# Order of GpSimd work, loads and background pieces in a fused attention and FFT kernel

## The chip, the cores and the metric

The kernel runs on one core of a Trainium2 chip. The metric is the device time of one execution in microseconds; before the change it is 700.23 us, the median of three runs (699.89 to 700.64).

## The reference

Two independent results are concatenated. The first is a causal attention over four segments of 512 positions, 32 heads of 18, with a memory that is carried from segment to segment:

```python
logits = jnp.einsum("bhqd,bhkd->bhqk", qs, ks) * scale + mask
p = _softmax(logits, axis=-1)
a_dot = jnp.einsum("bhqk,bhkd->bhqd", p, vs)
pq = phi(qs)
num = jnp.einsum("bhld,bhde->bhle", pq, M)
den = jnp.einsum("bhld,bhd->bhl", pq, z)[..., None] + 1e-6
o = g * (num / den) + (1.0 - g) * a_dot
M = M + jnp.einsum("bhld,bhle->bhde", phi(ks), vs)
z = z + jnp.einsum("bhld->bhd", phi(ks))
```

and then `o @ wo` over all heads. The second result is a 2D real FFT of a 2048 x 576 array, a product with complex weights, and the inverse transform.

## The kernel before

The program is one stream of instructions per engine, in the order in which the Python code records them. First come the forward FFT, the projections of q, k and v with the middle of the FFT, and the inverse FFT; the last half, from about 350 us on, is the loop of `attention`, and all the edits lie there.

**The loop.** It has 133 steps t. A step handles one head of one segment: `k,hh=divmod(t,4)` makes groups of four heads k = 0 to 31, and eight groups (32 steps) are a segment g. In step t three things are interleaved on TensorE:

- `s1(t+11)`: the logits of a head eleven steps ahead, only for their row maxima. Matmuls L678, with the causal mask added by L691, reduced on VectorE (L686, L692).
- `s2(t)`: the logits of this head again, transposed and with the maxima subtracted in the matmul (L727, L731, L732, L736), and the exponentials on ScalarE into the tiles P[0], P[1], P[2] (L728, L733, L737).
- `pv`: the product of P with the values for the group of four heads before, in the second step of a group the blocks of P[0] and the last columns of P[1], in the fourth step the rest of P[1] and P[2] (L756).

**The zeros.** After the last head of a group, four `affine_select` on GpSimd (L741) put zeros above the causal diagonal, each on a 128 x 4 x 128 block of P.

**The maxima's parts.** In the first step of a group, `mpath(k+2)` takes the maxima of the group two further on, combines them (L704, L705) and splits them on GpSimd into two bf16 parts, the tile `mh` (L707, L708). In the second step TensorE transposes mh (L711), ScalarE copies the result (L714), and two steps after the split's step a small DMA in ScalarE's own instruction order (L717) writes it into two rows of the Q tile, where s2 will use it.

**Background pieces.** `bg` is a list of generators: first `late_setup`, which loads wo and splits it into a high part (copy on ScalarE, L649) and a low part `wol` (subtraction on GpSimd, L650); then for each later segment `den` (the denominators, L807, L810), `mixed` and `oproj`, the output projection of the segment before (L901, its PSUM copied by L903). `mixed` alternates two kinds: `combine` multiplies the stored outputs u by the spread reciprocals (a small matmul pb, L878, with the product on VectorE, L881 or L883), adds the memory's part on GpSimd (L884) and splits the sum (L863, L868); `mem1` computes the memory's numerator (matmul pn, L831, copied by L833) and multiplies it with a reciprocal (pb, L837, L838). pb, pn, the denominators and the output projection share one PSUM buffer named "post" during the loop. A step gives pieces twice: `run_bg(0)` early and `run_bg(1.2)` after pv. Each call adds its rate to an account and runs one piece if that holds one, so that a step has one piece, and one in five steps two.

**Loads.** They go through SyncE's one queue in the order of the code. `stack_dmas` loads Q and K of eight heads at a time (L660, L662), one entry of a list per step; `load_v` loads their values `vs` (L669); `pq_load` loads the rows of phi(q) for the memory (L801), for the first time in steps 16 to 20, and `den` of step 34 needs all five. Each DMA signals one of eight semaphores in turn, and a DMA's issue waits until the one before it on the same semaphore has landed.

Of the kernel before, what the change touches and what calls it, by code (L numbers as in the profile page):

```python
# [5 lines left out]
F32=mybir.dt.float32; F32R=mybir.dt.float32r  # L6
# [358 lines left out]
ORD=(4,0,1,2,3)  # L365
# [42 lines left out]
class ATT:  # L408
# [224 lines left out]
    def late_setup(s,cp):  # L633

        nc,io=s.nc,s.io; q=[]
        s.sel=cp.tile([96,5,126],BF,name="sel",bufs=1); nc.gpsimd.dma_start(s.sel,io["sel"].rearrange("p (t m) -> p t m",t=5))
        s.woh=cp.tile([128,5,576],F32R,name="woh",bufs=1); s.wol=cp.tile([128,5,576],F32R,name="wol",bufs=1)
        for t in (0,1,2,3,5,4,6):
            if t: yield
            if t<6:  # L640
                x=cp.tile([128,576],F32,name="ob"); q.append((t,x))
                nc.sync.dma_start(x,io["wo"][:,576*t:576*t+576])
            yield
            if t!=5: yield
            if len(q)>(t<6):
                u,x=q.pop(0)
                if u==5: nc.scalar.copy(s.wol[64:96,4],x[64:96]); continue
                r=128 if u<4 else 72
                nc.scalar.copy(s.woh[:,u],x)  # L649
                nc.gpsimd.tensor_tensor(s.wol[:r,u],x[:r],s.woh[:r,u].bitcast(F32),op=OP.subtract)  # L650
        yield
        yield from s.gates()
    def stack_dmas(s,n,qk):
# [65 lines left out]
    def s2(s,t):  # L719
        nc=s.nc; k,hh=divmod(t,4); n,qd=divmod(k,2); h=4*qd+hh  # L720
        Q,K=s.Qs[n%3],s.Ks[n%4]; tp=s.tp
        if hh==0: s.P[k]=[tp.tile([128,4,w],F32,name=f"P{i}") for i,w in enumerate((512,512,256))]
        P=s.P[k]
        q=lambda o: Q[:110,h,o:]
        kk=lambda j: K[:110,h,128*j:128*j+128]
        p0=s.ps.tile([128,512],F32,name="s2",tag="s2")
        nc.tensor.matmul(p0,kk(0),q(0),start=True,stop=True)  # L727
        nc.scalar.activation(P[0][:,hh],p0,AF.Exp,scale=SC)  # L728
        yield
        p1=s.ps.tile([128,512],F32,name="s2",tag="s2")  # L730
        nc.tensor.matmul(p1[:,:384],kk(1),q(128),start=True,stop=True)  # L731
        nc.tensor.matmul(p1[:,384:],kk(3),q(384),start=True,stop=True)  # L732
        nc.scalar.activation(P[1][:,hh],p1,AF.Exp,scale=SC)  # L733
        yield
        p2=s.ps.tile([128,256],F32,name="s2",tag="s2")
        nc.tensor.matmul(p2,kk(2),q(256),start=True,stop=True)  # L736
        nc.scalar.activation(P[2][:,hh],p2,AF.Exp,scale=SC)  # L737
        r=slice(0,4) if k<31 else (slice(0,3) if hh==2 else slice(3,4))
        if hh==3 or k==31 and hh==2:
            def sel(x):  # L740
                nc.gpsimd.affine_select(out=x[:,r],in_=x[:,r],pattern=[[0,r.stop-r.start],[1,128]],compare_op=OP.is_ge,fill=0.0,base=0,channel_multiplier=-1)  # L741
            sel(P[0][:,:,:128])
            sel(P[1][:,:,:128])
            sel(P[1][:,:,384:])
            sel(P[2][:,:,:128])
        yield
    def pv(s,k,jj):

# [91 lines left out]
        yield  # L840
    def mixed(s,g):

        c=s.combine(g-1)
        d=5 if g==3 else 4
        for i in range(5+d):
            next(c,None); yield
            if i>=d:
                for _ in s.mem1(g,ORD[i-d]): yield
    def ux_load(s,g,t):
        r=126 if t<4 else 72  # L850
        s.ux[t]=s.tp.tile([128,512],F32,name="ux",tag="ux",bufs=3)
        s.nc.sync.dma_start(s.ux[t][:r],s.uD[g][126*t:126*t+r])
    def combine(s,g):
# [19 lines left out]
        for t in range(7+late):  # L873
            if t>1 and not late: high(ORD[t-2]); low(ORD[t-2])
            if t<5:
# [3 lines left out]
                if g==0:  # L879
                    s.am[t]=tp.tile([126,512],F32,name="am",bufs=5)  # L880
                    nc.vector.tensor_tensor(s.am[t][:r],x[:r],pb[:r],op=OP.mult)  # L881
                else:
                    nc.vector.tensor_tensor(x[:r],x[:r],pb[:r],op=OP.mult)  # L883
                    eng().tensor_tensor(s.am[t][:r],x[:r],s.am[t][:r],op=OP.add)  # L884
# [54 lines left out]
    def begin(s,sm,sp,ps1):  # L939
        s.late=[]; s.now=-1  # L940
        s.sm,s.sp,s.ps1=sm,sp,ps1
        s.mh=sm.tile([128,8,16],BF,name="mh",bufs=1); s.nc.gpsimd.memset(s.mh,0.0)
        s.mg={};s.mx={};s.m2={};s.P={};s.vs={};s.rc={};s.am={};s.pq={};s.ux={};s.potag=None
    def prologue(s):

        nc,io=s.nc,s.io
# [18 lines left out]
    def attention(s,tp,ps):  # L965
# [7 lines left out]
        q=[]  # L973
# [11 lines left out]
        for t in range(133):  # L985
            k,hh=divmod(t,4); n,qd=divmod(k,2); g=k//8
            if hh==0 and qd==0:
                if 0<n<14: q+=s.stack_dmas(n+2,0)
                if 0<n<13: q+=s.stack_dmas(n+3,1)
                if n+2<16: q.append(lambda n=n: s.load_v(n+2))  # L990
            st=t%32
            if 16<=t<21: s.pq_load(1,ORD[t-16])
            if t==34: bg.append(s.den(1,lane))
            if st==8 and g>0:
                def ln(g=g):
# [18 lines left out]
            steps(a,1)  # L1014
            steps(b,1)
            if 4<=t-1<132: s.pv((t-5)//4,(t-5)%4)
            run_bg(1.2)
            steps(a,1)
            if hh==1 and m is not None: steps(m,1)
            steps(b,1)  # L1020
            if hh==1 and m is not None: steps(m,1)
            if hh==0 and k+2<32: m=s.mpath(k+2); next(m)
            if t>=7 and t%4==3:
                s.pv_out((t-7)//4)
                if t%8==3:
# [155 lines left out]
```

## Time and profile before

| | |
|---|---|
| median of three runs | 700.23 us |
| profiled execution | 701.5 us, its span on the core 699.8 us |
| attention loop and tail | about 350 us to the end |
| GpSimd's selects L741 | 132, 78.2 us in all |

The span is the time from the first to the last instruction in the trace; the rest of an execution's time lies around it. Engines: PE is TensorE, PEld its weight loads, DVE VectorE, ACT ScalarE, POOL GpSimd, SP SyncE; a "q" behind a name means the engine's issuing of a DMA. Idle time of an engine is put down to what ended it. The profile models where a matmul ends, so matmuls that follow each other overlap.

### The profile page before, as it was taken

What the parts mean: (1) busy time and instruction counts of PE and PEld (TensorE: products, weight loads), DVE (VectorE), ACT (ScalarE), POOL (GpSimd) and SP (SyncE); (2) the same over time, 40 slices, a digit from 0 to 9 for tenths busy, and PEclk for the clock granted to TensorE, in tenths of its full rate; (3) what the DMA queues carried; (4) which work ended last, traced back from release to release, by engine and by line L of the source; (5) the groups of instructions that cost most, each with busy time, mean ns of one, the idle gap of its engine ahead of it and who ended that gap; (6) DMA issues with size and microseconds to landing.
All of it is one profiled execution on the core that took longest, in us unless ns stands there. A gap on an engine that the chain in (4) does not pass through costs nothing.

```text
span 699.8 us, 14371 instructions
## 1 busy us (share of the span) xinstructions
PE 680.0 (97%) x5040; PEld 501.9 (72%) x5040; DVE 537.7 (77%) x1149; ACT 445.3 (64%) x997; POOL 192.3 (27%) x389
## 2 busy tenths in 40 slices
PE   8999899999999999999999899999999999998998
PEld 5999679879879879999954455445666445663497
DVE  5898989789689679798588788888667876567633
ACT  4786695584684574545387687777656776567531
POOL 2111000100200101665135343443323652235310
PEclk9999999999999999999999999999999999999999
DMA  9895355594465778999348876986666776442142
GB/s 335 279 316 179 111 162 190 154 268 155 130 191 190 171 213 297 206 231 250 130 124 193 182 172 153 197 196 161 148 141 166 200 161 154 101 132 67 29 152 90
DMA packets 71362, 123.81 MB, mean 177 GB/s; under 512 B 12236, under 2 KB 39530, under 8 KB 67698
## 3 DMA queue, kind: packets, MB, share of 16 engines
q1 hardware_dynamic: 64638, 106.89, 58.0%
q0 software_dynamic: 5632, 15.76, 8.3%
q8 instruction: 40, 0.66, 0.4%
q10 hardware_dynamic: 1020, 0.25, 0.2%
q14 instruction: 32, 0.26, 0.1%
HBM read 82.10 MB, written 39.81 MB: 174 GB/s over the span
## 4 chain that ended last, share of the span: by engine, by line
PE 83%; DVE 6%; DMA 3%; ACT 3%; POOL 2%; issue 2%; ACTq 0%; SPq 0%; DVEq 0%; POOLq 0%
PE pj L485 15%; PE s L678 10%; PE pv L756 10%; PE pjv L485 9%; PE po L901 6%; PE i L318 4%; PE i L329 4%; PE s L727 3%; PE f L145 3%; PE s L731 3%; PE c L166 3%; PE po L930 2%; PE s L691 2%; PE pn L831 2%; PE pm L553 2%
## 5 line engine op out<-in xcount | busy, mean ns | idle before, releaser
L686 DVE CUSTOM_DVE_ANT_0 junk<-s,x 128x512 bf16<-128x512 f32 x248 | 137.0, 552 | 56.0 <-PE s L678 50.9
L741 POOL TENSOR_SCALAR_AFFINE_SELECT P<-P 128x512 f32<-128x512 f32 (+2 forms) x132 | 78.2, 623 | 112.4 <-ACT P L728 104.6
L692 DVE TENSOR_REDUCE mx<-s 128x4 f32<-128x512 f32 x128 | 87.7, 685 | 6.2 <-PE s L691 3.9
L728 ACT ACTIVATE P<-s 128x512 f32<-128x512 f32 x128 | 77.9, 609 | 12.3 <-PE s L727 3.4
L756 PE MATMUL pv<-P,vs 128*32 128x512 f32 (+3 forms) x1024 | 82.5, 439 | 0.1
L737 ACT ACTIVATE P<-s 128x256 f32<-128x256 f32 x128 | 50.0, 391 | 46.3 <-PE s L736 46.0
L733 ACT ACTIVATE P<-s 128x512 f32<-128x512 f32 x128 | 77.8, 608 | 2.5 <-PE s L732 2.2
L678 PE MATMUL s<-Ks,Qs 108*128 108x384 bf16 (+3 forms) x256 | 69.2, 301 | 1.5 <-DVE mx L692 1.2
L756 PEld LDWEIGHTS pv<-P,vs 128*32 128x32 f32 x1024 | 26.9, 109 | 45.3 <-issue 34.9
L485 PE MATMUL pj<-x,wqkh 128*128 128x512 f32 x162 | 56.4, 408 | 0.0
L230 DVE TENSOR_TENSOR Z<-Z 128x580 f32<-128x580 f32 (+2 forms) x51 | 45.6, 911 | 0.5
L678 PEld LDWEIGHTS <-Qs 108*128 108x128 bf16 x320 | 31.5, 98 | 19.3 <-issue 9.2
L691 PE MATMUL s<-tri,idb 128*128 128x128 bf16 x256 | 43.0, 219 | 0.0
L543 POOL MEMSET vt<- 128x32 f32 x16 | 2.3, 161 | 139.1 <-PE pm L553 127.8
L318 PE MATMUL i<-civ,Y 128*128 128x256 f32 (+1 forms) x288 | 39.2, 288 | 0.2 <-POOL Y L303 0.2
L318 PEld LDWEIGHTS i<-civ,Y 128*128 128x128 f32 (+1 forms) x288 | 36.6, 181 | 0.9 <-POOL Y L303 0.4
L329 PE MATMUL i<-itab,T 128*128 128x290 f32 (+1 forms) x224 | 36.6, 306 | 0.1
L485 PEld LDWEIGHTS pj<-x,wqkh 128*128 128x128 f32 x162 | 30.4, 189 | 8.5 <-issue 2.0
L485 PE MATMUL pj<-xh,wqkl 128*128 128x512 f32 x90 | 35.6, 395 | 0.0
L485 PE MATMUL pj<-xh,wqkh 128*128 128x512 f32 x90 | 35.6, 395 | 0.0
L485 PE MATMUL pj<-x,wqkl 128*128 128x512 f32 x90 | 35.5, 395 | 0.0
L504 DVE SCALAR_TENSOR_TENSOR ex<-pj,ex 128x512 f32<-128x512 f32 (+1 forms) x28 | 19.3, 689 | 20.2 <-ACT ex L502 20.1
(216 smaller groups left out, 1805.9 us busy)
## 6 DMA issues: line engine op xcount, KB each, us to landing
qkD<-sp SPq DMA_DIRECT2D x32, 384.0 KB
xin<-xb SPq DMA_DIRECT2D x16, 384.0 KB
cfw<-cfw POOLq DMA_DIRECT2D x16, 384.0 KB, 5.5
civ<-civ POOLq DMA_DIRECT2D x16, 384.0 KB, 9.7
vs<-vD SPq DMA_DIRECT2D x16, 330.0 KB
vD<-vt SPq DMA_DIRECT2D x16, 311.0 KB
W<-w SPq DMA_DIRECT2D x16, 290.0 KB
yb<-yout SPq DMA_DIRECT2D x16, 290.0 KB
```

The source lines that it names most:

```text
L318: nc.tensor.matmul(p[:m,k],Y[i][:,q,c*128:c*128+m],cc[:,hl,o:o+256],start=n==0,stop=n==5)
L329: nc.tensor.matmul(p,x,t,start=n==0,stop=n==6)
L485: s.nc.tensor.matmul(out,a,b,start=i==0,stop=i==len(L)-1)
L678: nc.tensor.matmul(out,Q[:108,h,128*i:128*i+128],K[:108,h,:128*(i+1)],start=True,stop=True)
L686: nc.vector.tensor_tensor_reduce(out=junk[:,:w],in0=src,in1=s.mask[:,512-w:],scale=1.0,scalar=-3.0e38, op0=OP.add,op1=OP.max,accum_out=s.m ...
L691: nc.tensor.matmul(pa[:,o+w-128:o+w],s.idb,s.tri,start=False,stop=True,skip_group_check=True)
L692: nc.vector.tensor_reduce(out=s.mx[k][:,hh],in_=pa.rearrange("p (b c) -> p b c",c=128),axis=mybir.AxisListType.X,op=OP.max)
L728: nc.scalar.activation(P[0][:,hh],p0,AF.Exp,scale=SC)
L733: nc.scalar.activation(P[1][:,hh],p1,AF.Exp,scale=SC)
L737: nc.scalar.activation(P[2][:,hh],p2,AF.Exp,scale=SC)
L741: nc.gpsimd.affine_select(out=x[:,r],in_=x[:,r],pattern=[[0,r.stop-r.start],[1,128]],compare_op=OP.is_ge,fill=0.0,base=0,channel_multiplie ...
L756: nc.tensor.matmul(s.pvt[32*hh:32*hh+32,128*j:],vt[:,j,19*h:19*h+32],mv[0][:,hh,mv[1]],start=j==0,stop=j>1,skip_group_check=True)
```

## The change

Five things:

1. Of the four selects only two (P[0] and the last columns of P[1], which pv reads first) stay at the end of a group. The other two are kept in `s.rest` and recorded in the next step, behind `mpath`. For the last group all four stay together.
2. The subtraction for `wol` is recorded a step after its copy, and `late_setup` gets one more pause per tile. The addition of `combine` for segment 1 moves to the end of its step where it would fall in the first step of a group.
3. The background rate is 1.0 during `mixed` of segments 1 and 2, 1.35 after it, and 1.2 at the start and during `mixed` of segment 3.
4. The first pq loads are in steps 18, 21, 24, 27 and 30.
5. `load_v` is placed seventh in the list of eight stack loads, not behind it.

```diff
-                nc.gpsimd.tensor_tensor(s.wol[:r,u],x[:r],s.woh[:r,u].bitcast(F32),op=OP.subtract)
+                s.later(1,lambda u=u,x=x,r=r: nc.gpsimd.tensor_tensor(s.wol[:r,u],x[:r],s.woh[:r,u].bitcast(F32),op=OP.subtract))
+                yield
...
             sel(P[0][:,:,:128])
-            sel(P[1][:,:,:128])
             sel(P[1][:,:,384:])
-            sel(P[2][:,:,:128])
+            def rest():
+                sel(P[1][:,:,:128])
+                sel(P[2][:,:,:128])
+            if k<31: s.rest=rest
+            else: rest()
...
     def mixed(s,g):
+        s.rate=1.0 if g<3 else 1.2
...
+        if g<3: s.rate=1.35
...
-                    eng().tensor_tensor(s.am[t][:r],x[:r],s.am[t][:r],op=OP.add)
+                    f=lambda t=t,x=x,r=r,e=eng(): e.tensor_tensor(s.am[t][:r],x[:r],s.am[t][:r],op=OP.add)
+                    f() if eng() is nc.vector or s.now%4<3 or g==2 else s.later(1,f)
...
-                if n+2<16: q.append(lambda n=n: s.load_v(n+2))
+                if n+2<16: q.insert(6,lambda n=n: s.load_v(n+2))
...
-            if 16<=t<21: s.pq_load(1,ORD[t-16])
+            if t in (18,21,24,27,30): s.pq_load(1,ORD[(18,21,24,27,30).index(t)])
...
-            run_bg(1.2)
+            run_bg(s.rate)
...
+            if hh==0 and s.rest: s.rest(); s.rest=None
```

`s.later(n,f)` records f at the end of the step n steps after the last finished one.

What this does to the instruction order, at the three places that matter below. Lines of the changed kernel are up to eight higher than those before. First GpSimd, from the end of the second group of heads on. Before:

```order
L741 AFFINE_SELECT P_4403<-P_4403 128x4x128
L741 AFFINE_SELECT P_4404<-P_4404 128x4x128 x2
L741 AFFINE_SELECT P_4405<-P_4405 128x4x128
L707 CAST mh<-mg 128x16
L708 TENSOR_TENSOR mh<-mg,mh 128x16
L650 TENSOR_TENSOR wol<-ob,woh 128x576 x2
```

and changed:

```order
L742 AFFINE_SELECT P_4401<-P_4401 128x4x128
L742 AFFINE_SELECT P_4402<-P_4402 128x4x128
L708 CAST mh<-mg 128x16
L709 TENSOR_TENSOR mh<-mg,mh 128x16
L742 AFFINE_SELECT P_4402<-P_4402 128x4x128
L742 AFFINE_SELECT P_4403<-P_4403 128x4x128
L650 TENSOR_TENSOR wol<-ob,woh 128x576
```

The three numbers are P[0], P[1] and P[2] of the group. Two of the four selects have moved behind the maxima's parts, and one of two subtractions for wol to a later place.

Second SyncE's queue around the first pq loads, in steps 15 to 19. Before:

```order
L801 DMA pq<-pqD_78 72x512
L660 DMA Qs_3134<-qkD_71 48x4096
L660 DMA Qs_3134<-qkD_71 32x4096
L801 DMA pq<-pqD_78 126x512
L660 DMA Qs_3134<-qkD_71 16x4096
L801 DMA pq<-pqD_78 126x512
L662 DMA Qs_3134<-reD_75 12x4096
L801 DMA pq<-pqD_78 126x512
```

and changed, from the first pq load on:

```order
L805 DMA pq<-pqD_78 72x512
L663 DMA Qs_3134<-reD_75 12x4096
L661 DMA Ks_3136<-qkD_71 48x4096
L661 DMA Ks_3136<-qkD_71 32x4096
L771 DMA rD_3147<-U 4x2x512
L776 DMA uD_3143<-U 18x2x512
L805 DMA pq<-pqD_78 126x512
L670 DMA vs<-vD_82 128x4x165
```

Only the first, smaller pq load is now ahead of the last piece of Q (from reD); the second comes behind the first pieces of K and the first stores of the outputs.

Third TensorE in step 56, the first of a group, in `mixed` of segment 1. Before:

```order
L727 MATMUL s_6336<-Qs_3134,Ks_3138 128x512
L878 LDWEIGHTS sel
L878 MATMUL pb<-rr,sel 126x512
L678 LDWEIGHTS Qs_3135
L678 MATMUL s_6347<-x_2607,Qs_3135 128x512
L731 LDWEIGHTS Ks_3138
L731 MATMUL s_6351<-Qs_3134,Ks_3138 128x384
L732 LDWEIGHTS Ks_3138
L732 MATMUL s_6351<-Qs_3134,Ks_3138 128x128
L831 MATMUL pn<-pq,Mst_64 126x512
```

and changed:

```order
L728 MATMUL s_6334<-Qs_3134,Ks_3138 128x512
L679 LDWEIGHTS Qs_3135
L679 MATMUL s_6337<-x_2607,Qs_3135 128x512
L732 LDWEIGHTS Ks_3138
L732 MATMUL s_6341<-Qs_3134,Ks_3138 128x384
L733 LDWEIGHTS Ks_3138
L733 MATMUL s_6341<-Qs_3134,Ks_3138 128x128
L884 LDWEIGHTS sel
L884 MATMUL pb<-rr,sel 126x512
```

The step had two pieces, pb in the early slot and pn in the late one; it now has pb alone in the late slot, and pn follows in step 57. The order holds the same number of pieces before the loop's end.

More of the change, by code (lines that the diff above doesn't have):

```diff
@@ L942, in begin @@
         s.mh=sm.tile([128,8,16],BF,name="mh",bufs=1); s.nc.gpsimd.memset(s.mh,0.0)
-        s.mg={};s.mx={};s.m2={};s.P={};s.vs={};s.rc={};s.am={};s.pq={};s.ux={};s.potag=None
+        s.mg={};s.mx={};s.m2={};s.P={};s.vs={};s.rc={};s.am={};s.pq={};s.ux={};s.rate=1.2;s.potag=s.rest=None
     def prologue(s):
```

## The prediction

> **What bounds the kernel now.** I read the page first, then the busy times stretch by stretch, then who TensorE waits for, then the timeline at each of those waits.
>
> ```profile
> PE 680.0 (97%) x5040; PEld 501.9 (72%) x5040; DVE 537.7 (77%) x1149; ACT 445.3 (64%) x997; POOL 192.3 (27%) x389
> ```
>
> TensorE is busy for 97% of the 699.8 us, so what can be won is idle time between matmuls. All edits lie in the attention loop, which begins at about 350 us. The next view is the busy time of the engines in stretches of it (PE, PEld, DVE, ACT, POOL with the number of instructions, then the granted clock, the DMA share and GB/s).
>
> ```profile
> core 0: us, PE busy (x) PEld busy (x) DVE busy (x) ACT busy (x) POOL busy (x), PEclk, DMA share, GB/s
> 360.00:404.00 44.00, 40.48 (x369) 20.30 (x365) 34.54 (x109) 34.06 (x83) 20.84 (x37) 1.00 0.80 174
> 404.00:440.00 36.00, 36.00 (x349) 18.70 (x345) 30.41 (x95) 28.08 (x69) 11.45 (x25) 1.00 0.75 159
> 440.00:458.00 18.00, 16.86 (x162) 8.51 (x162) 16.22 (x47) 14.28 (x36) 8.42 (x19) 1.00 0.92 205
> 458.00:484.00 26.00, 25.12 (x205) 12.38 (x198) 21.60 (x63) 19.43 (x45) 12.15 (x22) 1.00 0.74 178
> ...
> 545.00:584.00 39.00, 37.43 (x302) 18.74 (x295) 31.40 (x91) 28.74 (x67) 23.20 (x34) 1.00 0.77 177
> ...
> 634.00:661.00 27.00, 24.68 (x186) 10.19 (x183) 18.35 (x35) 18.53 (x44) 13.26 (x23) 1.00 0.21 58
> ```
>
> The clock is full everywhere. From 404 to 440 us TensorE never rests: the loop is bound by matmuls there, and nothing that only reorders other engines can win time. Idle are 44.00 - 40.48 = 3.5 us in 360 to 404, 1.1 in 440 to 458, 0.9 in 458 to 484, 1.6 in 545 to 584 and 2.3 in 634 to 661; behind that lies a tail that the change does not touch. Two rows of the PE timeline give the floor of four loop steps with no background piece: the first matmul of steps 28 and 32.
>
> ```profile
> 409.32 0.38 PE L727 MATMUL s<-x,Ks 110*128 110x512 bf16 x1
> 417.11 0.38 PE L727 MATMUL s<-Qs,x 110*128 110x512 bf16 x1
> ```
>
> That is 7.79 us; a group of four steps without pieces that takes longer has stalled. Who TensorE waited for between 355 and 700 us (total, times, longest):
>
> ```profile
> PE mt L711 <- POOL mh L708: 2.5, 5, 0.8
> PE s L727 <- ACT P L728: 1.7, 6, 0.5
> PE s L678 <- DVE mx L692: 1.0, 1, 1.0
> PE s L678 <- DVE mg L704: 1.0, 1, 1.0
> PE pn L831 <- DVE am L881: 0.7, 1, 0.7
> ...
> PE pn L831 <- DVE ux L883: 0.6, 1, 0.6
> PE pb L878 <- DVE ux L883: 0.5, 1, 0.5
> ...
> PE pb L878 <- DVE am L838: 0.3, 1, 0.3
> ```
>
> **Part one, half of the zeros behind the maxima's parts.** The costliest wait is for the maxima's parts mh. Step 8 in the timeline:
>
> ```profile
> 366.38 2.40 POOL L741 TENSOR_SCALAR_AFFINE_SELECT P<-P 128x512 f32<-128x512 f32 x4
> 368.72 0.20 POOL L707 CAST mh<-mg 128x16 bf16<-128x16 f32 x1
> 368.62 0.28 PE L678 MATMUL s<-Ks,Qs 108*128 108x256 bf16 x1
> 369.28 0.23 PE L711 MATMUL mt<-idb,mh 128*128 128x128 bf16 x1 [0.38 <-POOL mh L708]
> ```
>
> Four selects of 0.60 us stand ahead of mh on GpSimd, and the transpose L711, with all of TensorE's work behind it, waits for mh. The change leaves two selects ahead: mh starts 1.20 us sooner, at 367.5, and L711, which starts 369.28 - 368.72 = 0.56 us after mh does, could start at 368.1. The matmul before it is issued at 368.62, so the wait is gone with 0.5 us to spare. A wait costs a little more than its idle time, as a matmul's modelled end runs past the start of the next, here of two that wait for nothing:
>
> ```profile
> 468.13 0.27 PE L678 MATMUL s<-x,Qs 108*128 108x256 bf16 x1
> 468.24 0.27 PE L736 MATMUL s<-x,Ks 110*128 110x256 bf16 x1
> ```
>
> The first counts as busy for 0.27 us but is followed after 0.11, so 0.16 us are added for each wait. Five waits: 2.5 + 5 x 0.16 = 3.3 us, the upper bound. No wait is over 0.8 us idle, less than the 1.20 moved. The later ones also have additions ahead of mh, of which the change moves some behind it:
>
> ```profile
> L884 POOL TENSOR_TENSOR am<-ux,am 126x512 f32<-126x512 f32 (+1 forms) x8 | 10.1, 1269 | 2.9 <-DVE ux L883 2.9
> ```
>
> I take 3.0. Lower bound nothing, if another wait stands right behind. The two moved selects cost nothing: they are read by the third quarter of pv, three steps later, and even lean steps take 7.79 / 4 = 1.9 us on average, so 5.8 us cover them, with 1.2 us needed. Without that cover each group of four steps would pay up to 1.2 us.
>
> **Part two, pq loads apart, values sooner.** The SP queue, ACT and PE at steps 16 to 21:
>
> ```profile
> 383.13 0.35 SPq L801 DMA_DIRECT2D pq<-pqD x1
> 385.58 0.29 SPq L662 DMA_DIRECT2D Qs<-reD x1
> 391.13 0.62 ACTq L717 DMA_DIRECT2D x<-mts x1
> 392.44 0.38 PE L727 MATMUL s<-Qs,Ks 110*128 110x512 bf16 x1 [0.46 <-ACT P L728]
> 394.55 0.32 PE L678 MATMUL s<-x,Qs 108*128 108x384 bf16 x1 [1.01 <-DVE mg L704]
> ```
>
> The small DMA of L717 sits in ACT's own order, so the exponential L728 stands behind it, and TensorE's L727, which needs that exponential's buffer, 1.3 us behind the issue. In the program this issue waits for the semaphore of the pq load of step 16 (issued at 383.13), so that load took 8.0 us to land. The second wait, at 394.55, is the first matmul on the Q of the next eight heads. The timeline names L704, but the program has no such dependence: that matmul's weights wait for the loads of Q, the last of which was issued at 385.58 behind three pq loads. Three of 252 KB at 174 GB/s (the first stretch) are 4.3 us. In the change one pq load is ahead instead of three, so Q is 2.9 us earlier against a wait of 1.0, and L717's predecessor is a Q load of step 15. Upper bound: 0.46 + 1.01 + 2 x 0.16 = 1.8 us; lower bound nothing, if the backlog lasts even so. I take 1.5, since most pq bytes leave the stretch. The vs load three steps sooner waits for a pv that is by then done: nothing.
>
> The Trainium skill ("DMA: Bandwidth & Descriptors", section "Issuing engines are not separate DMA queues") says that DMAs run on the same 16 engines whichever engine issued them. By that rule nothing is saved, the bytes only move: the DMA share is 0.80 before 404 us and 0.75 after, so the trace agrees that the later stretch is no emptier. By that rule alone this part would bring 0 of its 1.5 us, and the loads would meet their reader later (the third rival).
>
> **Part three, one background piece in a step.** At rate 1.2 a step sometimes holds two pieces, and both use the one PSUM buffer "post", as here in step 56:
>
> ```profile
> 469.07 0.38 PE L878 MATMUL pb<-rr,sel 96*126 96x512 bf16 x1
> 469.88 0.67 DVE L881 TENSOR_TENSOR am<-ux,pb 126x512 f32<-126x512 f32 x1
> 470.61 1.12 PE L831 MATMUL pn<-pq,Mst 126*126 126x512 f32 x2 [0.73 <-DVE am L881]
> ```
>
> pn needs the buffer that DVE gives back 1.5 us after pb. At rate 1.0 the next piece is a step away. The order of the changed program has no step with pb and pn together, nor two pb of the combining in one, at the places of all four such waits: 0.7 (L881), 0.6 and 0.5 (L883) and 0.3 (L838). With 0.16 each: 2.1 + 0.6 = 2.7 us, upper bound. The pieces held back are made up at rate 1.35 among output projections, where six steps instead of five hold two (about 0.2 us for the one more, by the 0.16 above). I take 2.3; lower bound -0.5, if the made-up pairs stall as the old ones did once.
>
> **Part four, wol later.** This subtraction stands on GpSimd right before the selects:
>
> ```profile
> 373.75 1.41 POOL L650 TENSOR_TENSOR wol<-ob,woh 128x576 fp32r<-128x576 f32 x1 [0.40 <-ACT woh L649]
> ```
>
> Spread over more steps, it and its ACT copies collide less; of the "L727 <- ACT P L728" row 0.3 us falls here. I take 0.3, between nothing and 0.5. Its reader, the first output projection, comes some 45 steps later.
>
> **Sum.** 3.0 + 1.5 + 2.3 + 0.3 = 7.1 us, less 0.6 for waits that were hidden behind these (of the exponentials after 634 us, and the pairs) = 6.5 us. The profiled span becomes 699.8 - 6.5 = 693.3; that execution took 701.5 us in all, the median of the runs is 700.23, so I predict 700.23 - 6.5 = **693.7 us**. The 1.0 us of L692 (two reciprocals behind each other) and the tail stay. All upper bounds give 3.3 + 1.8 + 2.7 + 0.5 = 8.3. The idle time of the four stretches concerned, 3.5 + 0.9 + 1.6 + 2.3 = 8.3, with 0.16 for each of some 14 waits in them, is 10.5 at most. Between the two lies 9.5: 690.7.
>
> **Rivals.** First, the waits only move. ACT and DVE have 34.1 and 34.5 us of work in a stretch that would shrink from 44 to 40.5, so 85% each, and 16.22 of 18.00 us on DVE at 440: little slack. Then perhaps half arrives: 700.2 - 3.3 = 697.0. Against it: in 404 to 440 DVE had 30.41 of 36.00 us, the same 85%, and TensorE never waited.
>
> Second, no change, 699.9: the moved GpSimd work slows DVE beside it, and mh waits for DVE instead. The trace speaks against it. L692 in the 2.4 us of four selects, and in the free stretch 404 to 440:
>
> ```profile
> L692 DVE TENSOR_REDUCE mx<-s 128x4 f32<-128x512 f32 x1 | 0.7, 681 | 0.0
> L692 DVE TENSOR_REDUCE mx<-s 128x4 f32<-128x512 f32 x18 | 12.4, 688 | 0.5
> ```
>
> Third, slower: the last pq load, now asked for at step 30 and not 20, is late for its reader, the denominators' matmul in step 34, and TensorE stands. The four steps last 7.8 us; one load under load took 8.0 us, and if its issue waits for another on the same semaphore, as L717's did, 16 us: 8.2 us lost against 6.5 won, 701.9. It decides from a landing 14.3 us after step 30 on. Against it: after 404 us the share is 0.75, and four groups of four steps ran there without a wait.
>
> Fourth, more than I think, 690.7, if every bound is reached.
>
> **How the numbers follow.** Forecast 58%, moved waits 16%, no change 8%, slower 9%, more 9%. Within 0.2% (1.4 us) is what a measurement of this kernel can't tell from no change. Faster by more than that: 58 + 16 + 9 = 83%; same 8%; slower 9%. The range from 690.4 to 698.6 takes in the forecast, the first and the fourth rival, with the sum of the lower bounds of all parts but the first (700.2 - 3.0 + 0.5, and 0.9 more for half of the L727 row growing again) at its upper end.
>
> **What would show it.** Right: no wait of L711 for mh, POOL rows with two selects, mh, two selects; the stretch of steps 7 to 24 shorter by about 4 us; no wait over 0.3 us of L831 or L878; L728 not behind an idle ACT at step 18; L807 unwaited in step 34. Wrong: "L727 <- ACT P L728" or "L678 <- DVE" grown by what L711 lost, or waits of L807 for pq.

## The result and the profile after

The changed kernel takes 699.0 us (median of 22 runs, 696.28 to 701.79) against 700.3 us before (22 runs, 699.08 to 701.97): a ratio of 0.9974, 95% interval 0.9964 to 0.9984, 1.1 to 2.5 us faster. 693.7 was forecast, a gain of 6.5. The profiled execution took 699.54 us, 2.0 less than the one of before, and its page shows the same work:

```profile
PE 679.3 (97%) x5040; PEld 501.7 (72%) x5040; DVE 537.3 (77%) x1149; ACT 444.7 (64%) x997; POOL 191.4 (27%) x389
```

The same stretches as in the prediction (busy us of PE, PEld, DVE, ACT, POOL, then the granted clock, the DMA share and GB/s), after:

```profile
360.00:404.00 44.00, 42.34 (x399) 22.04 (x398) 37.22 (x118) 36.91 (x91) 22.50 (x39) 1.00 0.77 173
404.00:440.00 36.00, 35.89 (x341) 18.35 (x340) 30.73 (x94) 28.01 (x69) 12.46 (x26) 1.00 0.80 168
440.00:458.00 18.00, 16.91 (x153) 8.65 (x151) 15.95 (x48) 14.18 (x37) 7.87 (x18) 1.00 0.92 197
458.00:484.00 26.00, 25.16 (x207) 12.67 (x211) 21.91 (x65) 19.96 (x48) 11.26 (x20) 1.00 0.85 197
545.00:584.00 39.00, 37.31 (x307) 18.47 (x306) 31.10 (x91) 28.98 (x69) 24.08 (x36) 1.00 0.72 175
```

In the first stretch TensorE's idle time has fallen from 3.5 to 1.7 us; in 440 to 458, 458 to 484 and 545 to 584 it is what it was (1.1, 0.8, 1.7). Who TensorE waits for between 355 and 700 us, after:

```profile
PE s L679 <- DMA pq<-pqD: 1.7, 1, 1.7
PE s L679 <- DMA Qs<-reD: 1.5, 1, 1.5
PE s L679 <- DVE mx L693: 1.0, 1, 1.0
PE s L728 <- ACT P L729: 1.0, 4, 0.3
PE po L908 <- DVE am L837: 0.8, 1, 0.8
PE s L679 <- DVE mg L687: 0.7, 1, 0.7
PE mt L712 <- POOL mh L709: 0.6, 1, 0.6
```

(L679 was L678, L728 was L727, L712 was L711.) The waits that the change was aimed at are gone: for mh 0.6 is left of 2.5, for the exponentials 1.0 of 1.7, and L835 and L884 (pn and pb, before L831 and L878) are not in the list, 2.1 us before. But L679, the maxima's logits, waits 1.7 + 1.5 + 0.7 = 3.9 us besides the 1.0 that was left alone, where before one wait of 1.0 stood. The names behind the arrows differ, the instruction does not: each is the first matmul on the Q of the next eight heads, in steps 21, 93 and 53. Step 21 in the timeline:

```profile
381.67 0.32 SPq L661 DMA_DIRECT2D Qs<-qkD  x1
...
383.03 0.77 SPq L661 DMA_DIRECT2D Qs<-qkD  x2
383.84 0.39 SPq L805 DMA_DIRECT2D pq<-pqD  x1
...
384.27 0.37 SPq L663 DMA_DIRECT2D Qs<-reD  x1
...
392.31 0.32 PE L679 MATMUL s<-x,Qs 108*128 108x384 bf16 x1 [1.66 <-DMA pq<-pqD]
```

By the program this matmul needs the four Q loads, and nothing of pq.

Step 8 shows the wait for mh that is gone, on GpSimd and TensorE:

```profile
364.87 1.22 POOL L742 TENSOR_SCALAR_AFFINE_SELECT P<-P 128x512 f32<-128x512 f32 x2 [1.30 <-ACT P L729]
...
368.99 0.20 POOL L708 CAST mh<-mg 128x16 bf16<-128x16 f32 x1 [2.89 <-DVE mx L693]
369.27 0.22 POOL L709 TENSOR_TENSOR mh<-mg,mh 128x16 bf16<-128x16 f32 x1
...
369.65 0.22 PE L712 MATMUL mt<-idb,mh 128*128 128x128 bf16 x1
```

Two selects end at 366.1, mh waits 2.89 us for VectorE and then TensorE not for mh.

A table of stages says where that leaves the loop: us from the first matmul of L727 (L728) of the stage's first step to that of the next stage, worked out from the timelines of before, after, and three of the runs below.

| steps | before | after | before, no Q (e6) | after, no Q (e5) | after, no K (e14) |
|---|---|---|---|---|---|
| 0 to 7 | 14.97 | 14.98 | 14.97 | 14.97 | 14.98 |
| 8 to 19 | 27.11 | 23.38 | 26.03 | 23.37 | 23.37 |
| 20 to 51 | 66.63 | 67.07 | 65.41 | 65.39 | 65.53 |
| 52 to 83 | 86.77 | 87.28 | 86.76 | 86.68 | 86.66 |
| 84 to 115 | 88.12 | 88.06 | 88.14 | 86.45 | 86.46 |
| 116 to 123 | 16.87 | 16.87 | 16.86 | 16.88 | 16.86 |
| together | 300.47 | 297.64 | 298.17 | 293.74 | 293.86 |

The change wins 3.73 us by step 20, runs at the floor (three groups at 7.79) there, loses 0.95 in steps 20 to 83, and wins nothing more. The loop is 2.83 us shorter; 0.89 of that the profiles lose because the loop of after begins that much later (351.25 against 350.36 us), behind a program that is the same: over the twenty kernels here it begins anywhere from 348.95 to 351.61. So parts are measured below by the loop of their profile, and the kernels by their runs.

The runs show one thing that this table can't. The granted clock, averaged over an execution, was 0.996 to 0.998 in 9 of the changed kernel's 22 runs, and their median is 699.86 us; in the other 13 it was 0.999 or 1.000, and their median is 697.92. The profile of after is one of the 13: its clock is full through the whole loop, so all that stands above is won and lost by waits alone. What takes the clock away in the nine is not in a trace of this kernel, but traces of others below show such stretches (e3, e16, e17), each behind a wait of TensorE.

**Theory A**, formed from this: the stalls are really removed, but TensorE then reaches the next Q sooner than its loads land, and the gain is given back there. **The rival**: the gain is given back in many small places (exponentials, pairs of pieces). Ratios below are against runs of the kernel before on the same chip; its median there was 700.57 us (e1 to e4), 700.85 (e5 to e8), 700.94 (e9 to e12), 700.88 (e13 to e16) and 701.82 (e17, e18). The expectations count a wait from start to start of two matmuls, about 0.16 us more than the idle time in the lists: 1.83, 0.90 and 1.62 us there are 1.7, 0.7 and 1.5 here.

### The profile page after: what moved, and what is told of

It reads as the page before. It is cut to its first block, busy times and chain, and to the rows that moved or that the text cites. A ratio compares the mean times of both kernels' runs of the same rounds, so it can differ in the third digit from the quotient of the medians.

```text
span 697.8 us, 14377 instructions
## 1 busy us (share of the span) xinstructions
PE 679.3 (97%) x5040; PEld 501.7 (72%) x5040; DVE 537.3 (77%) x1149; ACT 444.7 (64%) x997; POOL 191.4 (27%) x389
## 4 chain that ended last, share of the span: by engine, by line
PE 85%; DVE 5%; DMA 3%; ACT 3%; issue 2%; POOL 1%; SPq 0%; DVEq 0%; ACTq 0%; POOLq 0%
PE pj L485 15%; PE s L679 10%; PE pv L760 10%; PE pjv L485 9%; PE po L908 6%; PE i L318 4%; PE i L329 4%; PE s L728 4%; PE f L145 3%; PE s L732 3%; PE c L166 3%; PE po L937 2%; PE s L692 2%; PE pn L835 2%; PE pm L553 2%
## 5 line engine op out<-in xcount | busy, mean ns | idle before, releaser
L679 PE MATMUL s<-Ks,Qs 108*128 108x384 bf16 (+3 forms) x256 | 69.1, 301 | 3.0 <-DMA Qs<-reD 1.5
L679 PEld LDWEIGHTS <-Qs 108*128 108x128 bf16 x320 | 31.5, 98 | 21.9 <-issue 10.0
```

The costliest lines, as they stand in the source:

```text
L679: nc.tensor.matmul(out,Q[:108,h,128*i:128*i+128],K[:108,h,:128*(i+1)],start=True,stop=True)
```

## Experiments: the parts alone

Each of three is the kernel before with one part of the change.

**e1**, the selects split (`sel(P[1][:,:,:128])` and `sel(P[2][:,:,:128])` behind `mpath`), nothing else.

> The kernel before with only two of the four selects moved behind the maxima's parts. Theory A (what is won ahead of the next heads' Q is given back there, since the loads of Q take a fixed time from their issue): the waits of L711 in steps 8 to 20 go (2.0 us), but the first matmul on the Q of step 21 then waits about 2.5 to 3 us instead of 1.2, so the time falls by 0.3 to 1.0 us. Theory B (my prediction's part one stands by itself): the time falls by 3.0 us, and the wait in step 21 stays at 1.2.

Measured: 701.65 us, ratio 1.0017 (1.0002 to 1.0031): slower, where both expectations had a gain. Steps 8 to 19 fell from 27.11 to 25.45, steps 20 to 51 grew from 66.63 to 68.99. Its waits show why:

```profile
PE s L678 <- DMA uD<-U: 1.8, 1, 1.8
...
PE s L678 <- DMA Ks<-qkD: 1.5, 1, 1.5
PE mt L711 <- POOL mh L708: 1.2, 2, 0.8
```

The waits for mh are halved, and L678 waits on the Q of steps 21 and 29. More is given back than was won.

**e2**, the pq loads spaced.

```diff
-            if 16<=t<21: s.pq_load(1,ORD[t-16])
+            if t in (18,21,24,27,30): s.pq_load(1,ORD[(18,21,24,27,30).index(t)])
```

> The kernel before with only the first pq loads three steps apart. Theory A: the wait of the first matmul on Q in step 21 falls from 1.2 to under 0.4 us and L727's of 0.6 us in step 20 goes: 1.2 to 1.8 us faster. Theory B' (the bytes only move, and the loads in steps 21 to 30 are as much in the way): within 0.5 us of the kernel before.

Measured: 699.53 us, ratio 0.9977 (0.9963 to 0.9991), the loop 298.40 against 300.47. The wait of step 21 is gone. By itself, with TensorE no earlier than before, this part does what was forecast.

**e3**, the rates alone (1.0 in `mixed`, 1.35 after).

> The kernel before with only the rates 1.0 and 1.35. Theory A: the waits of L831 and L878 for the shared buffer go (2.5 us), but the first matmul on Q in step 93 waits 1 us or more, in step 53 0.5 us more, and pieces in the late slot behind pv cost 0.5 us in each of two segments: within 0.7 us of the kernel before. Theory B (part three of the prediction): 2.3 us faster.

Measured: 703.27 us, ratio 1.0032 (1.0016 to 1.0049): slower, which neither expectation had. The waits of pn and pb are gone, and in their place stands the largest row of its list:

```profile
PE mt L711 <- POOL mh L708: 4.8, 6, 1.5
```

With one piece in each step a `combine` piece falls into more of the steps in which mh is due, and GpSimd has an addition ahead of mh beside the four selects. The loop is 2.72 us longer than before, 2.81 of it in steps 116 to 123, and the waits are not all of that: behind the wait of 1.5 us for mh in step 117 the granted clock is 0.50 for 3.4 us, which by itself costs up to 1.7. Nine of the twelve runs have a clock below 0.999; the median of the other three is 701.66, 1.2 above the 700.50 of the kernel before at such a clock.

## Experiments: where the gain went

**e5** and **e6**: the loads of Q inside the loop are left out, of the changed kernel and of the one before (the matmuls then read what the buffer holds from earlier, so only the time means anything; the same holds for e14, e15, e16 and e18).

```diff
-                if 0<n<14: q+=s.stack_dmas(n+2,0)
+                if 0<n<14: q+=[lambda: None]*3+[lambda n=n: s.loaded.add((n+2,0))]
```

> The changed kernel without the loads of Q inside the loop (from the Q of heads 24 to 31 on; the score matmuls read what the buffer holds from earlier, so the output is not the reference's). Theory A (what the change frees is given back where the first matmul of eight heads waits for its Q): the waits of 1.83, 0.90, 0.22 and 1.62 us in steps 21, 53, 85 and 93 of the changed kernel go, 4.6 us, so 699.0 - 4.6 = 694.4, and no wait stands at those steps. Rival (the gain is given back in many small places: exponentials, pairs of pieces among output projections): once Q is there, the next thing is late, and the time stays at 697.5 or above.

> The kernel before without the loads of Q inside the loop (output not the reference's). Theory A: only the wait of step 21 (1.18 us, with 0.22 at step 53) was Q's before, so 700.3 - 1.4 = 698.9; against the changed kernel without these loads, the change is then worth 4.5 us instead of 1.8. Rival (Q's loads cost time in both kernels alike, for instance by taking DMA time from others): both kernels gain about the same, and the change stays worth about 2 us.

Measured: 695.02 us (4 runs, ratio 0.9921, 0.9901 to 0.9941) and 699.62 us (0.9992, 0.9979 to 1.0004). Without Q's loads the change is worth 699.62 - 695.02 = 4.6 us, by the loops 4.43, with them 2.83. The waits of e5:

```profile
PE s L679 <- DVE mx L693: 1.0, 1, 1.0
PE s L728 <- ACT P L729: 1.0, 4, 0.3
PE po L908 <- DVE am L837: 0.8, 1, 0.8
PE mt L712 <- POOL mh L709: 0.6, 1, 0.6
PE po L908 <- ACT ob L910: 0.4, 1, 0.4
```

All three waits that the list of after gave to a pq load, a Q load and VectorE went with Q's loads, and nothing took their place: theory A, not the rival. But removing a load also frees the DMA engines, and that leaves two causes: Q asked for late, or landing late.

**e4**: the changed kernel with the four Q loads asked for together, in the first step of eight, and none of the stack's loads in the next two.

```diff
-            if q: q.pop(0)()
+            if q and not (n<14 and n>0 and t%8 in (1,2)): q.pop(0)()
...
-            if q and t%8==0: q.pop(0)()
+            for _ in range(3 if t%8==0 else 0):
+                if q: q.pop(0)()
```

> The changed kernel with the four loads of Q all asked for in the first step of eight, and no load in the next two steps. Theory A: the waits of the first matmul on Q in steps 21, 53 and 93 (1.83, 0.90 and 1.62 us in the changed kernel's profile) fall to under 0.4 us each; 3 to 4 us faster than the changed kernel, 4.5 to 5.5 faster than before. Theory C (these waits are VectorE's, as the timeline names them): the same waits, and the time of the changed kernel, 1 to 2 us faster than before.

Measured: 696.36 us, ratio 0.993 (0.9908 to 0.9953), the loop 295.70. Of the 3.9 us before L679, 1.4 are left, 0.9 of them at step 21, though there the four loads of Q are issued within 2 us.

**e14**: the changed kernel as it is, without the loads of K inside the loop; Q's stay in their steps.

```diff
-                if 0<n<13: q+=s.stack_dmas(n+3,1)
+                if 0<n<13: q+=[lambda: None]*3+[lambda n=n: s.loaded.add((n+3,1))]
```

> The changed kernel without the loads of K inside the loop (from the K of heads 32 to 39 on; output not the reference's); Q's loads stand where the change has them, in the same steps. Theory A (Q is late because the DMA engines are busy with what is around it): with K's 885 KB out of every eight steps the waits of 1.83, 0.90 and 1.62 us in steps 21, 53 and 93 fall below 0.3 each, 694.8. Rival (Q is asked for too late, whatever else is on the DMA engines: its steps and its place in SP's order set its landing): the waits stay at 1 us or more each, and the time above 697.

Measured: 694.81 us, ratio 0.9908 (0.9883 to 0.9932), the loop 293.86, which is that of e5 within 0.12. Q is in time though it is asked for in the same steps. The stretch around step 21, of before, after and e14 in turn:

```profile
380.00:392.00 12.00, 10.83 (x99) 5.29 (x98) 9.20 (x33) 8.12 (x21) 4.16 (x7) 1.00 0.97 202
```

```profile
380.00:392.00 12.00, 10.65 (x103) 5.43 (x101) 10.29 (x34) 10.61 (x26) 5.40 (x9) 1.00 0.94 200
```

```profile
380.00:392.00 12.00, 11.87 (x113) 6.10 (x111) 10.37 (x34) 10.89 (x28) 4.90 (x12) 1.00 0.68 146
```

With the DMA engines busy for 0.97 or 0.94 of the time Q lands late; at 0.68 TensorE is busy for all but 0.13 us. Nor is Q asked for earlier: its last load is issued 6.9 us before that matmul's start in e14, 8.0 us in after. So it is the DMA engines' load that holds Q.

**e9**: e8 below with K's loads held back to steps 5 to 7 of eight, and the values in step 3.

```diff
-                if n+2<16: q.insert(6,lambda n=n: s.load_v(n+2))
+                if n+2<16: q.insert(4 if 0<n<13 else 6,lambda n=n: s.load_v(n+2))
...
-            if q and not (n<14 and n>0 and t%8 in (1,2)): q.pop(0)()
+            if q and not (n<14 and n>0 and t%8 in (1,2,4)): q.pop(0)()
...
-            for _ in range(3 if t%8==0 else 0):
+            for _ in range({0:3,6:1}.get(t%8,0)):
```

> The version with Q early and pq late, and the loads of K held back from the steps behind Q's to steps 5 to 7 of eight (values in step 3). Theory A1 (Q lands late because K's packets of 8 KB, issued right behind, share the DMA engines with it): the wait at step 21 falls from 1.04 to below 0.4 us, that of step 93 from 0.31 to 0.1, and the time to 695.1. Rival A2 (Q's own 885 KB take that long from the step on in which the buffer is free): the wait stays at 1.0, the time at 696.0. Lost, if K or the values are late in their turn: a wait elsewhere in steps 13, 21, 29.

Measured: 703.97 us, ratio 1.0038 (1.0017 to 1.0059), 7 us slower than e8 by the ratios. At step 21 the wait, 0.9 us idle in e8, is gone, as A1 has it; but K's loads now stand ahead of the next Q, and its list has waits for Q in steps 93, 45 (0.6 of the 1.6, the rest is the two reciprocals), 53 and 29:

```profile
PE s L679 <- DMA pq<-pqD: 2.7, 1, 2.7
PE s L679 <- DVE mg L687: 1.6, 1, 1.6
PE s L679 <- DMA vs<-vD: 1.3, 1, 1.3
...
PE s L679 <- DMA rD<-U: 0.7, 1, 0.7
```

With e14: the loads can be reordered, but a load that is held back is held into the next one's time. This profile was the fastest of twelve runs (699.68; the slowest 708.31) and the only one at a full clock: the others had 0.990 to 0.998. A span times what its clock lacks of 1 is the time lost to it at most, on average 3.2 us of these twelve runs. So a good part of the 7 us is not waiting but half speed, and how long those eleven waited is not known.

## Experiments: what each part is worth

With Q's loads out, no wait for Q hides what a part frees.

**e15**, e5 with the rate 1.2 throughout (the two lines that set `s.rate` in `mixed` left out).

> The changed kernel without the loads of Q (695.0 us) and with the background pieces at rate 1.2 throughout: what pacing is worth when nothing of Q's loads stands behind it. Theory A: the waits of pn and pb come back, and 1.6 us slower, 696.6 (0.5 in steps 52 to 83, 1.1 in steps 84 to 115). Rival (made-up pairs among the output projections lose what the mixed steps win): 695.3 or less. Output not the reference's.

Measured: 695.7 us, ratio 0.9925 (0.9901 to 0.9949); the loop is 295.42 against e5's 293.74, 1.68 longer, 0.63 of it in steps 52 to 83 and 1.07 in 84 to 115, where theory A put it. The runs' medians, on different chips, differ by 0.7 only, and the two spans by 0.4, as the part behind the loop took 1.4 us longer in e5's profile, for which no cause was found. Back in its list:

```profile
PE pn L835 <- DVE am L885: 0.7, 1, 0.7
PE pn L835 <- DVE ux L887: 0.7, 1, 0.7
...
PE pb L882 <- DVE ux L887: 0.5, 1, 0.5
...
PE pb L882 <- DVE am L842: 0.3, 1, 0.3
```

**e7**, the same with Q's loads in, e4 at the rate 1.2 throughout.

> The version with Q asked for in one step, but with the background pieces at rate 1.2 throughout. Theory A (pacing is worth something once selects and additions are behind mh and Q is in time): the four waits of pn and pb (0.73, 0.6, 0.5, 0.3 us with their overlap) come back in part, 1.2 to 2.1 us slower than the paced one at 696.4, so 697.6 to 698.5. Rival (what pacing wins in the mixed steps, the made-up pairs among output projections lose): 696.4 within 0.5.

Measured: 697.66 us, ratio 0.9959 (0.9945 to 0.9973), but the loop 296.14 against 295.70: of the 1.68 only 0.44 show, as the paced kernel waits for Q in step 93 where this one does not. The runs are 1.3 us slower than e4's by the medians and 2.0 by the ratios, but on different chips and with intervals of 1.0 and 1.6 us either way, so they can't decide between 0.4 and the 1.2 that theory A had at least.

**e16**, e5 with all four selects and the additions ahead of mh again.

> The changed kernel without the loads of Q (695.0 us), with all four selects and the additions ahead of the maxima's parts again, as before. Theory A (part one is worth what its waits show): waits for mh of 2.1 us in steps 8 to 19 and 1.0 us or more in steps 84 to 100 come back, 3.1 us slower or a little more, 698.1 to 698.8. Rival (other waits stand right behind the one for mh): 1 us slower or less, 696.0. Output not the reference's.

Measured: 699.75 us, ratio 0.9986 (0.9968 to 1.0003), 4.7 slower than e5, more than theory A had, and in another place. Steps 8 to 19 take 23.37 us, the floor; the loss lies in steps 84 to 91 and 116 to 119, 2.1 and 2.7. Step 8 on GpSimd and TensorE:

```profile
365.64 1.81 POOL L742 TENSOR_SCALAR_AFFINE_SELECT P<-P 128x512 f32<-128x512 f32 x3
...
369.17 0.20 POOL L708 CAST mh<-mg 128x16 bf16<-128x16 f32 x1 [1.72 <-DVE mx L693]
369.45 0.22 POOL L709 TENSOR_TENSOR mh<-mg,mh 128x16 bf16<-128x16 f32 x1
369.62 1.40 POOL L650 TENSOR_TENSOR wol<-ob,woh 128x576 fp32r<-128x576 f32 x1
```

The selects stand ahead of mh, and mh still waits 1.72 us for VectorE. What has gone from its front is the subtraction for wol, which ran at 365.02 before, in the way of the selects. Around step 84, where an addition stands behind the selects, they do hold it:

```profile
543.47 2.39 POOL L742 TENSOR_SCALAR_AFFINE_SELECT P<-P 128x512 f32<-128x512 f32 x4
...
545.83 1.26 POOL L887 TENSOR_TENSOR am<-ux,am 126x512 f32<-126x512 f32 x1
547.03 0.19 POOL L708 CAST mh<-mg 128x16 bf16<-128x16 f32 x1
...
547.58 0.23 PE L712 MATMUL mt<-idb,mh 128*128 128x128 bf16 x1 [1.36 <-POOL mh L709]
```

Not all of the 2.7 in steps 116 to 119 is theirs. Behind a wait of 1.47 us for mh in step 117 the granted clock is 0.50 from 638.3 to 641.7 us, up to 1.7 us lost; e5 waits 0.63 there and keeps its clock. Nine of e16's twelve runs are below 0.999, and the median of the other three is 698.5, 3.5 above e5.

**e18** and **e17**: the kernel before with only wol's subtraction later, without Q's loads and with them.

```diff
-                nc.gpsimd.tensor_tensor(s.wol[:r,u],x[:r],s.woh[:r,u].bitcast(F32),op=OP.subtract)
+                s.later(1,lambda u=u,x=x,r=r: nc.gpsimd.tensor_tensor(s.wol[:r,u],x[:r],s.woh[:r,u].bitcast(F32),op=OP.subtract))
+                yield
```

> As e17, without the loads of Q inside the loop (output not the reference's). Theory W: the groups of steps 8 to 19 fall from 26.0 (the kernel before without these loads) to 23.4 us, and all of it arrives: 699.6 - 2.6 = 697.0. Rival: 699.0 or above.

> The kernel before, with only wol's subtraction one step later and its pieces spread. Theory W (in steps 8 to 19 it was the 1.41 us subtraction ahead of the four selects that held mh, not the selects themselves): the three groups of steps 8 to 19 fall from 27.1 to 23.4 us, Q's wait at step 21 grows from 1.18 to about 2.5 and at step 29 to 1.5, so 2 us or less arrive, 698.5 to 700.3. Rival (the selects alone hold mh): the groups stay above 26 us, the time at 700.3.

Measured: e18 696.38 us, ratio 0.993 (0.9914 to 0.9945), steps 8 to 19 at 23.37 instead of 26.03: this one edit brings 2.7 us. With Q's loads, e17: 702.11 us, ratio 1.0004 (0.9991 to 1.0018), nothing. Steps 8 to 15 gain 1.7 us in its profile (the slowest of its twelve runs), and then:

```profile
380.46 0.50 SPq L802 DMA_DIRECT2D pq<-pqD  x1
...
392.27 0.62 ACTq L718 DMA_DIRECT2D x<-mts  x1
392.94 0.60 ACT L729 ACTIVATE P<-s 128x512 f32<-128x512 f32 x1 [5.07 <-DMA pq<-pqD]
393.44 0.59 ACT L734 ACTIVATE P<-s 128x512 f32<-128x512 f32 x1
393.59 0.58 PE L728 MATMUL s<-Qs,Ks 110*128 110x512 bf16 x1 [3.47 <-DMA Qs<-reD]
```

The small DMA in ScalarE's order waits for the pq load of step 16, now 11.8 us under way, ScalarE stands for 5 us behind it, and TensorE for 3.47: the chain of the prediction's part two, several times its size. And then TensorE runs at half its clock (the last three columns are the granted clock, the DMA share and GB/s):

```profile
388.00:392.00 4.00, 2.12 (x25) 0.94 (x23) 2.50 (x8) 0.00 (x0) 0.00 (x0) 1.00 1.00 209
392.00:396.00 4.00, 2.41 (x11) 1.27 (x11) 1.21 (x5) 3.03 (x7) 2.39 (x4) 0.61 0.94 171
396.00:400.00 4.00, 4.00 (x25) 1.29 (x24) 1.44 (x4) 2.02 (x6) 1.78 (x4) 0.54 0.80 188
400.00:404.00 4.00, 4.00 (x39) 2.08 (x38) 3.71 (x14) 2.98 (x8) 1.26 (x3) 1.00 0.54 151
```

The clock is 0.50 from 392.9 to 399.7 us, 6.8 us, and TensorE, busy for all but 0.7 of them, takes longer for the same work: the matmul of L728 takes 0.58 us there and 0.38 in the profile of before. All twelve runs of e17 have a clock of 0.994 to 0.998, on average 3.1 us lost, against 0.6 for the kernel before on that chip. So "nothing" is a gain that was paid back twice, in waiting and in half speed; without the clock's share e17 would be some 2 us faster than the kernel before, by an estimate from these means (702.12 - 3.09 against 701.56 - 0.58).

## Experiments: making room

**e8**: e4 with the pq loads in steps 22, 24, 26, 28, 30.

> The version with Q asked for in one step, and pq loads in steps 22, 24, 26, 28, 30 instead of 18, 21, 24, 27, 30. Theory A (Q of step 21 is late because of what lies ahead of it on the DMA engines): the pq loads of steps 18 and 21 no longer share with Q, so the wait of 1.06 us at step 21 falls below 0.4 and the time by 0.7, to 695.7. Rival (Q's own loads take that long from the step in which the buffer is free): the wait stays at 1.06, the time at 696.4. Lost, if pq is late for the denominators: a wait at step 34.

Measured: 696.04 us, ratio 0.9937 (0.9919 to 0.9954): as e4. The wait of step 21 stayed at 0.9 us: the pq loads were not what it had left to wait for (e9 shows that K's were), and the denominators were in time.

**e10**, **e11** and **e12** change e9, and suffer from its late Q. e10 moves the additions of the third combining too; e11 moves none; e12 is e10 at the rate 1.2.

> As e9, and GpSimd's additions are moved behind the maxima's parts in the third combining too, which the change leaves out. Theory A: the wait for mh of 0.84 us in step 117 goes, 0.7 faster than e9, 694.4. Rival (behind it the exponentials, ACT busy, are late at once): the same as e9 within 0.3.

> As e9, but no addition is moved (the diff's line with later is undone). Theory A (additions ahead of mh hold it, as the selects do): 0.5 to 1.0 us slower than e9, by waits for mh between steps 84 and 100. Rival (the two selects moved are enough): the same as e9 within 0.3.

> As e10, but at rate 1.2 throughout. Theory A (pacing is worth what its steps show once Q is in time): 1.6 us slower than e10, 0.5 in steps 52 to 83 and 1.1 in steps 84 to 115, with the waits of pn and pb back. Rival (pairs made up among output projections give it back): 0.4 or less.

Measured: e10 703.52 us, ratio 1.0033 (1.0012 to 1.0055); e11 701.47, 0.9994 (0.9976 to 1.0011); e12 706.94, 1.0077 (1.0051 to 1.0104). e10's steps 116 to 123 take 16.07 us instead of 16.88, the 0.8 of the wait for mh, yet its loop is longer: the Q wait of step 93 was 3.1 us against 2.7, and behind it the clock was 0.50 for 3.4 us, which costs more than the wait grew. In e11 steps 84 to 91 take 0.9 longer, so that moving the additions is worth that much there, and the Q wait behind them is 2.7 shorter. e12 says nothing on pacing, as the waits in steps 20 to 51 (70.74 us against 67.13) and two stretches at half clock, 3.4 and 6.8 us long, drown it. All three fail as tests of their part in the runs' times: under a late Q a faster kernel is not a faster run, by the waits and by the clock that their runs lost (0.989 to 0.998 in e10, 0.988 to 0.998 in e12).

**e13**: e8 with the additions of the third combining moved as well.

```diff
-                    f() if eng() is nc.vector or s.now%4<3 or g==2 else s.later(1,f)
+                    f() if eng() is nc.vector or s.now%4<3 else s.later(1,f)
```

> The version with Q early and pq late (696.0 us), and GpSimd's additions moved behind the maxima's parts in the third combining too. Theory A: the wait for mh of 0.84 us in step 117 goes, 0.7 faster, 695.3. Rival (the exponentials behind it are late at once, or the DMA engines give it back): 696.0 or above.

Measured: 695.53 us (6 runs, 695.29 to 696.64), ratio 0.992 (0.9898 to 0.9942). The wait of step 117 is gone (16.07 us in steps 116 to 123), and this version beats the kernel before by 5.4 us and the changed one by about 3.5. It keeps a wait of about 1 us for Q at step 21 and the 1.0 for two reciprocals.

## Why the prediction came out as it did

The direction was right and the size wrong, 1.3 to 1.8 us instead of 6.5. By its steps:

**Part one (3.0 us): the waits went, for a cause that was half misread.** Waits for mh fell from 2.5 to 0.6, and L712 is unwaited in step 8. But the quoted order, four selects and then mh, was read as the selects holding mh. With the subtraction for wol out of the way all four selects may stand ahead of mh in steps 8 to 19 at no cost (e16), and moving that subtraction alone brings the stage to its floor (e18). Splitting the selects alone gets 1.66 of 3.7 there (e1). The selects and additions matter in steps 84 to 119, with pacing: 4.8 us in the loop (298.57 of e16 less 293.74), up to 1.7 of it by the half clock behind the longest wait.

**Part four (0.3 us)** was therefore the worst-sized term: 2.7 us without Q's loads. Its row, 1.41 us right before the selects, stood in the prediction, costed for collisions with ScalarE and not for what queues behind it on GpSimd.

**Part two (1.5 us) is the step that failed.** It is right alone: e2 gained 1.6 us by its ratio and the wait of step 21 went. Its sentence "Q is 2.9 us earlier against a wait of 1.0" held TensorE's own time fixed. The whole change brings TensorE to step 20 3.7 us sooner, so by the prediction's own numbers the wait should have been 1.0 + 3.7 - 2.9 = 1.8; it measured 1.66. (Of its "three of 252 KB" the first is 144 KB, so the three are 3.7 us and not 4.3; the two that moved, 2.9 us, stand.) In steps 53 and 93 the same wait arose where none of 0.3 us stood, because nobody asked when Q lands if TensorE comes sooner. The lower bound "nothing, if the backlog lasts even so" was too high: the term can be negative.

The Trainium skill ("DMA: Bandwidth & Descriptors", section "Issuing engines are not separate DMA queues") was read there as giving this part nothing, since bytes that move are served by the same 16 engines. For the part alone the measurement decides against that reading (1.6 us gained): e2 only moves bytes behind the load that is waited for, and the wait is gone. For the whole change the trace agrees that the engines stay as full: the DMA share around step 21 is 0.94 after and was 0.97 before, and only less traffic (e14, 0.68) or an earlier issue helped. No run here moved these loads to another issuing engine.

**Part three (2.3 us)**: the mechanism held, no wait of pn or pb is left, and 1.68 us is what it is worth without Q's loads (e15); with them 0.44 (e7). Alone it is slower, by 2.2 us by e3's ratio and 1.2 at the full clock: it needs part one, as it puts additions ahead of mh, which the prediction did not see because it read order and stalls of the program with all parts in.

**The sum.** With Q's loads out, the change wins 4.43 us in the loop, where the prediction without part two has 3.0 + 2.3 + 0.3 = 5.6; the 1.2 too many lie in steps 52 to 115 (1.77 won). Then Q's loads take 1.60 of it, where part two had 1.5 won: 7.1 - 1.2 - 3.1 = 2.8, the loop's 2.83. The 0.6 taken off for hidden waits named the exponentials and the pairs; the wait that was hidden was the one whose matmul the prediction had just identified. What is left between the loop's 2.8 and the 1.3 of the medians is in good part the clock, a term that the prediction did not have: on average 0.95 us of the 22 runs, and the 13 at 0.999 or 1.000 are 2.4 us below the kernel before. (The clock of that kernel's 22 runs is not on record; on the other chips its runs lost 0.2 to 0.6.)

**Rivals.** "The waits only move" was the true one, held at 16% and with too weak a price: it looked for slack on ScalarE and VectorE, which had enough (e5 runs at the floor with both), and not on the DMA engines, whose 0.80 and 0.92 stood in the quoted rows. GpSimd beside VectorE (no change) did not show; the late pq load did not come: the denominators of step 34 are unwaited.

**What was said to show it** went as said for pn, pb and step 34, and for mh but for the 0.6 us of step 117; steps 7 to 23 became 3.1 us shorter, not 4; the exponential behind L718's DMA waits 0.41 us for TensorE and for no load; and the "wrong" sign that the prediction itself named, "L678 <- DVE" grown, is what came, with DMA names beside it.

Still open is how the sixteen DMA engines divide their time between the loads, as the trace has no engine per packet, and what decides whether half a clock follows a wait. A version with fewer bytes of Q and K was not tried.

## What to carry to other kernels

A wait that is removed brings the engine sooner to the next buffer that is loaded, so each load's slack has to be taken against the new time, not the old; where the DMA share is as high as in the stretches where Q was late here (0.72 to 0.94), work out when the transfers alone would be done before adding up stalls. Terms of a change are not additive: alone, three parts here gave +1.2, -1.6 and +2.2 us by their ratios, and the whole change -1.8; leave out the suspected load in both kernels, and what is left is what the rest of the change is worth. What holds an instruction is often the operation two places ahead of it in its queue, so look at the whole front, not at the neighbour. And read the granted clock of every run beside its time: here it explains differences of 2 us and more that a profile at full clock doesn't show.

## What the runs showed of the hardware

- The same wait had a different name in each profile: the first matmul on Q in step 21 was put down to VectorE (before), a pq load (after) and the transfer of uD (e1). Only leaving Q's loads out, and K's, settled it.
- A wait of TensorE can be followed by half its clock. In the loops of the twenty profiles there are six such stretches, in e3, e10, e12 (two), e16 and e17, each at 0.50 for 3.4 or 6.8 us, and each begins before the end of a wait of 1.5 to 3.5 us or at most 2.4 us after it. The length of the wait does not decide it: 2.7 us in e9, 1.8 in e1 and 1.7 in after were followed by none.
- Runs scatter with the clock. The twelve runs of e9 span 8.6 us at clocks of 0.990 to 1.000, the six of e13 span 1.4, all at 1.000; the slowest run of the kernel before on each of the experiments' chips (703.2 to 704.8 us) had 0.994 to 0.998.
- A DMA issue in a compute engine's own order can stop that engine: ScalarE stood for 5.07 us (e17) behind one that waited for a load that had nothing to do with it.
